# Second part of x fetched in float32 by SyncE and cast by GpSimd, in a convolution and two-layer kernel

## The chip, the cores and the metric

The kernel runs on one core of one Trainium2 chip. The metric is the device time of one execution in microseconds (us), median of several runs; lower is better. The core's engines are TensorE (PE in the profile; PEld is its weight load), VectorE (DVE), ScalarE (ACT), GpSimd (POOL) and SyncE (SP). Transfers between device memory and on-chip memory run on 16 DMA engines. Requests that GpSimd issues appear on queue q0, those of SyncE on queue q1. PSUM is the memory into which TensorE writes.

## The reference, cut to what matters

Each of 8 sequences of 4096 rows of 192 numbers is convolved causally with 7 taps, one set of taps for each of 8 groups of 24 columns; the taps are a softmax. Then each of the 32768 rows goes through a product with w_in (192 by 2048), a leaky ReLU and a product with w_out (2048 by 192).

```python
w = np.exp(weight - max); w = w / (sum(w) + 1e-09)          # 8 heads x 7 taps
x_pad = zeros of 6 rows ahead of x                          # causal
out = np.einsum('hk,bskhg->bshg', w, x_unf)                 # the convolution
h = x @ w_in                                                # (32768, 2048)
g = np.maximum(0.01 * h, h)
return (g @ w_out).astype(np.float32)
```

Everything that a matrix product reads is bfloat16 on the chip; x and the weights arrive as float32.

## The kernel before

Sequences are taken in pairs: the two of a pair (called e = 0 and 1) share the 128 partitions, 64 columns of each in one chunk, with 3 chunks for the 192 columns. A block is 512 rows of a pair; there are 32 blocks. The first two blocks are split into halves of 256 rows, so the work is a list of 34 groups (line 72), the first four of them halves. For each group the kernel needs x transposed (columns on partitions, the tile xt), convolves it into yt, multiplies with w_in into PSUM (mm1, line 488; tile ph), applies the leaky ReLU on ScalarE into g (line 515), and multiplies with w_out (lines 525 and 588). The main loop (line 670) issues mm1 of group i beside the second product of group i-1 and the convolution of group i+1. One mm1 step is called u below; a half block has 8 of them.

The schedule is manual (line 67): every engine carries out its instructions in the order in which the code issues them, and waits come from data dependencies. One engine's instructions stay in that order, so an instruction that waits holds up all behind it on the same engine.

The start is special, since nothing is there to overlap with:

- Rows 0 to 255 of the first pair (part q = 0) are fetched by SyncE in float32 into x_nat (line 142, two requests), cast by ScalarE and VectorE (line 155) and transposed by TensorE (line 181).
- Part q = 1 (rows 256 to 511) is fetched by GpSimd with a cast on the way, into x_rows[1] (line 145, two requests, one for each e); part q = 2 likewise. TensorE transposes them against the identity (line 167). The twelve transposes of part 1 stand inside the very first mm1 step, between its second and third chunk (lines 501 and 502), and VectorE copies their result to xt (line 195).
- Part q = 3 is fetched by GpSimd in six requests (line 149) and transposed by DMA requests of SyncE (line 199).
- w_in comes in five requests of GpSimd (line 316): rows 0 to 127 of the first 1024 columns; then rows 128 to 191 of their nearer and their farther half; then the same two row ranges of the last 1024 columns. VectorE and ScalarE copy parts of it between the two halves of the partitions (spread_up and spread_down, lines 326 and 322), because mm1 needs them there. w_out comes in two requests (line 350).

GpSimd's order at the start is: a mask called sel, w_in rows 0 to 127, the identity (two instructions), w_in nearer half, the two requests of x part 1, three requests of w_in, two of x part 2, two of w_out, two small operations that make the tap weights wk (lines 445 and 446), the six requests of x part 3, and then x for the later blocks (line 96). VectorE uses wk first in the convolution of group 1 (line 222). SyncE's order is: two requests for x part 0, then the DMA transposes of part 3.

The pool stage_pool, from which x_nat comes, has two buffers; before the change one of them is used.

Of the kernel before, what the change touches and what calls it, by code (L numbers as in the profile page):

```python
# [10 lines left out]
FP32 = mybir.dt.float32  # L11
BF16 = mybir.dt.bfloat16
# [3 lines left out]
def kernel(  # L16
# [8 lines left out]
    nc = tc.nc  # L25

    B, S, D = x.shape
# [13 lines left out]
    HS = SUB // 2  # L41
    NFC = F // 128
# [3 lines left out]
    RUN = 4  # L46
# [10 lines left out]
    const_pool = ctx.enter_context(tc.tile_pool(name="const", bufs=1))  # L57
    stage_pool = ctx.enter_context(tc.tile_pool(name="stage", bufs=2))
# [17 lines left out]
    x_nat, x_bf, xt = {}, {}, {}  # L76

    def sync(after, first, why):
        tc.add_manual_dep(
            after.ins, first.ins.name,  # L80
            mybir.DependencyInfo(
                mybir.DependencyClass.Sync, mybir.DependencyReason.DATA
            ),
            reason=why,
        )
# [36 lines left out]
    def new_xt(rp):  # L122
# [10 lines left out]
    x_rows = {  # L133
        q: const_pool.tile([128, 2, HS, D], BF16, name=f"x_rows{q}") for q in (1, 2)
    }

    def load_first(q):
        rows = x[0:2, q * HT : (q + 1) * HT, :].rearrange("e (s p) d -> p e s d", s=HS)
        if q == 0:
            x_nat[q] = stage_pool.tile([128, 2, HS, D], FP32, name="x_nat")  # L140
            for s in range(HS):
                nc.sync.dma_start(out=x_nat[q][:, :, s], in_=rows[:, :, s])
        elif q in x_rows:
            for e in range(2):
                nc.gpsimd.dma_start(out=x_rows[q][:, e], in_=rows[:, e])  # L145
        else:
            for c in range(NCH):
                for e in range(2):
                    nc.gpsimd.dma_start(  # L149
                        out=x_half[q][:, c, :, e, :],  # L150
                        in_=rows[:, e, :, c * CH : (c + 1) * CH],
                    )

    def cast_first(q, s, copy, e=slice(0, 2)):
        copy(  # L155
            out=x_half[q][:, :, s, e, :],
            in_=x_nat[q][:, e, s, :].rearrange("p e (c k) -> p c e k", c=NCH),
        )
# [76 lines left out]
    def y_of(grp, c):  # L235
        blk, t0, T = grp
        if blk not in yt:
            yt[blk] = yt_pool.tile([128, NCH, ST], BF16, name="yt")
        return yt[blk][:, c, t0 : t0 + T]
# [47 lines left out]
    w9 = const_pool.tile([H, K + 1], FP32, name="w9")  # L287
    nc.scalar.dma_start(out=w9[:, 0:K], in_=weight)  # L288
    load_first(0)

    ones = nc.const_aps.tensor(1.0, [128, ST], BF16)
# [7 lines left out]
    for sign, off in ((1, 0), (-1, GRP - 1)):  # L299
        nc.gpsimd.affine_select(  # L300
            out=sel[:, :, 0, :], in_=sel[:, :, 0, :], compare_op=mybir.AluOpType.is_ge,
            fill=0.0, base=off, channel_multiplier=-sign * GRP,
            pattern=[[sign * CH, NCH], [sign, CH]],
# [10 lines left out]
    def load_w_in(n, rows, cols=slice(0, WF)):  # L314
        ps, slot = ((0, 128), 0) if rows == 0 else ((0, CH), 2)
        nc.gpsimd.dma_start(  # L316
            out=w_in[n][ps[0] : ps[1], slot, cols],
            in_=moe_w_in[rows : rows + ps[1], n * WF + cols.start : n * WF + cols.stop],
        )
# [15 lines left out]

    load_w_in(0, 0)
    ident = const_pool.tile([128, 128], BF16)
    make_identity(nc, ident)
    load_w_in(0, 128, near)
    load_first(1)  # L340
    load_w_in(0, 128, far)
    for rows in (0, 128):
        load_w_in(1, rows)
    load_first(2)


    w_out = const_pool.tile([128, NFC, D], BF16)
    for h in range(2):
        cs = slice(h * NFC // (2 * RUN), (h + 1) * NFC // (2 * RUN))
        nc.gpsimd.dma_start(  # L350
            out=w_out.rearrange("p (c i) d -> p c i d", i=RUN)[:, cs],
            in_=moe_w_out.rearrange("(c p i) d -> p c i d", p=128, i=RUN)[:, cs],
        )


    wa = psum_h.tile([128, 2, ST], FP32, name="warm", tag="ph")
# [1 line left out]
    def warm(n, cols=HT, to=wa[:, 0]):  # L358
# [10 lines left out]
        out=nmax, in_=w9[:, 0:K], axis=mybir.AxisListType.X,  # L369
# [3 lines left out]
        out=w9[:, 0:K], in_=w9[:, 0:K], func=mybir.ActivationFunctionType.Exp,  # L373
# [18 lines left out]
    def select(out, parts):  # L392
# [10 lines left out]
    wps_hm = wps_hm[:, :, 0]  # L403
    new_xt(0)
    cast_first(0, 0, nc.scalar.copy)
    cast_first(0, 1, nc.scalar.copy, slice(0, 1))
    cast_first(0, 1, nc.vector.tensor_copy, slice(1, 2))
    taps = const_pool.tile([128, NCH, 2, K + 1, 2], BF16, name="taps")
    nc.vector.tensor_copy(
        out=taps, in_=wps_hm[..., None].to_broadcast([128, NCH, 2, K + 1, 2])  # L410
# [5 lines left out]
    def diag_wide(c, p):  # L416
# [22 lines left out]
        out=rsum, in0=wml[:, :, K:], scalar=1e-9, in1=taps[:, :, 0, K:, 0],  # L439
# [14 lines left out]
    def act_scale(out, in_, scale):  # L454
# [11 lines left out]
        out=y_of(groups[0], 0), in0=hi[:, :HT], scalar=rsum[:, 0, :], in1=low,  # L466
# [301 lines left out]
```

## Time and the profile before

| What | Value |
|---|---|
| Runs of the kernel before | 681.44, 681.47 and 680.72 us, median 681.44 |
| Span of the profiled execution, first to last instruction | 679.2 us |
| Busy in that span: PE, ACT, DVE, POOL | 674.9, 517.6, 481.2, 147.4 us |
| Granted TensorE clock | 1.00 over the span |
| GpSimd's requests for x part 1, issued | from 3.62 us, 1.44 us for the two |
| The same, issue to landing | 3.9 and 3.7 us |
| SyncE's requests for x part 0, issue to landing | 2.6 us each |
| w_out, issue to landing | 7.7 us and 8.8 us |

The profiled execution's own time is its span and what lies around it; against the median of the runs, the part outside the span is 2.2 us. Times in the profile count from the first instruction. Of an instruction, the row of the timeline gives start, duration, engine, line, operation, the tile written and read, the number of instructions merged into the row and, in brackets, the idle time of the engine before it with what ended it.

### The profile page before, as it was taken

Reading aid. Unit: us, or ns where it says so; the run is one execution under the profiler, and the core shown is the slowest. Engines: PE = TensorE matmul, PEld = TensorE weight load, DVE = VectorE, ACT = ScalarE, POOL = GpSimd, SP = SyncE. Lnnn points to the kernel's source line nnn. Section 1 sums busy time; section 2 is a strip of 40 time slices with the busy share of each in tenths; the row PEclk is TensorE's granted clock in tenths of the full one; section 3 lists DMA queues with packets and bytes.
Section 4 is the critical chain, followed back from the end, with each engine's and each line's share of the span. In section 5 each row is a group of like instructions: output and inputs, shape, how many; then the busy total and the mean of one; then the engine's idle time right before and its main releaser. Section 6 shows DMA issues by size and latency. Waiting matters only on the chain.

```text
span 679.2 us, 27092 instructions
## 1 busy us (share of the span) xinstructions
PE 674.9 (99%) x12442; PEld 446.3 (66%) x12442; DVE 481.2 (71%) x816; ACT 517.6 (76%) x601; POOL 147.4 (22%) x208
## 2 busy tenths in 40 slices
PE   9999999999999999999999999999999999999998
PEld 6997666666666666666666666666666666666667
DVE  7989477866768766778667687667786676876612
ACT  7899877777787777777777777778777777777781
POOL 8455221122211222211222112222022220000000
PEclk9999999999999999999999999999999999999999
DMA  9999755655737656556556566567365573321123
GB/s 149 99 119 104 52 85 83 84 64 67 96 74 93 76 54 86 84 85 86 66 63 92 80 92 78 56 83 94 73 87 69 60 96 71 72 56 33 34 49 94
DMA packets 213970, 53.27 MB, mean 78 GB/s; under 512 B 209312, under 2 KB 213536, under 8 KB 213856
## 3 DMA queue, kind: packets, MB, share of 16 engines
q0 software_dynamic: 98832, 13.97, 30.3%
q1 hardware_dynamic: 115008, 37.57, 28.0%
q8 instruction: 97, 1.59, 0.9%
q14 instruction: 17, 0.14, 0.1%
q10 hardware_dynamic: 16, 0.00, 0.0%
HBM read 28.31 MB, written 25.17 MB: 79 GB/s over the span
## 4 chain that ended last, share of the span: by engine, by line
PE 98%; DVE 1%; ACT 0%; issue 0%; ACTq 0%
PE ph L507 49%; PE acc L588 44%; PE po L525 5%; PE acc L259 0%; DVE diag L420 0%; PE ptr L167 0%; ACT L366 0%; ACTq L288 0%; DVE w_in L322 0%; DVE yt L465 0%; DVE o_sb L638 0%; DVE x_half L155 0%; ACT w L372 0%; DVE w_in L326 0%; ACT junk L366 0%
## 5 line engine op out<-in xcount | busy, mean ns | idle before, releaser
L515 ACT ACTIVATE g<-ph 128x1024 bf16<-128x1024 f32 x512 | 496.6, 1021 | 139.8 <-PE ph L507 139.6
L228 DVE SCALAR_TENSOR_TENSOR yt<-xt,wk,yt 128x512 bf16<-128x512 bf16 (+1 forms) x582 | 380.1, 715 | 0.2
L507 PE MATMUL ph<-yt,w_in 64*64 64x512 bf16 (+2 forms) x6048 | 377.5, 369 | 0.3 <-DVE yt L465 0.3
L588 PE MATMUL acc<-g,w_out 64*64 64x512 bf16 x5568 | 339.9, 376 | 0.0
L507 PEld LDWEIGHTS <-w_in 64*64 64x64 bf16 (+1 forms) x6048 | 229.7, 131 | 103.4 <-issue 1.1
L588 PEld LDWEIGHTS <-w_out 64*64 64x64 bf16 x5568 | 178.2, 118 | 118.8
L96 POOL DMA_DIRECT2D x_bf<-in_x_dram x180 | 133.9, 774 | 407.6 <-DMA xt<-x_bf 405.6
L610 DVE STREAM_TRANSPOSE o_t<-acc 128x512 f32<-128x512 f32 x87 | 72.9, 875 | 182.2 <-PE acc L588 182.2
L525 PE MATMUL po<-w_out,g 64*128 64x192 bf16 (+1 forms) x640 | 36.8, 243 | 0.0
L525 PEld LDWEIGHTS <-g 64*128 64x128 bf16 (+1 forms) x640 | 32.6, 95 | 3.2 <-issue 0.4
L222 DVE TENSOR_SCALAR yt<-xt,wk 128x512 bf16<-128x512 bf16 (+1 forms) x97 | 28.8, 320 | 2.4 <-DMA xt<-x_bf 2.4
L598 ACT COPY junk<-junk 128x1 f32<-128x1 f32 x58 | 11.1, 191 | 4.1
L638 DVE COPY o_sb<-po 128x192 f32<-128x192 f32 x8 | 2.8, 356 | 6.8 <-PE po L525 3.9
L638 ACT COPY o_sb<-po 128x192 f32<-128x192 f32 x16 | 5.1, 323 | 0.3
L259 PE MATMUL acc<-xt,diag 64*64 64x256 bf16 x126 | 4.7, 272 | 0.1
L149 POOL DMA_DIRECT2D x_half<-in_x_dram x6 | 4.3, 732 | 0.9 <-DMA w_in<-in_moe_w_in_dram 0.9
L259 PEld LDWEIGHTS <-diag 64*64 64x64 bf16 x140 | 3.7, 106 | 1.0 <-issue 0.4
L360 PE MATMUL warm<-const-bfloat16-1.0 128*128 128x512 bf16 (+2 forms) x8 | 3.3, 577 | 0.8 <-PEq L752 0.8
L145 POOL DMA_DIRECT2D x_rows<-in_x_dram x4 | 2.9, 746 | 0.0
L316 POOL DMA_DIRECT2D w_in<-in_moe_w_in_dram x5 | 2.9, 593 | 0.0
L360 PEld LDWEIGHTS <-const-bfloat16-1.0 128*128 128x128 bf16 x10 | 1.2, 128 | 2.2 <-issue 2.2
L326 DVE COPY w_in<-w_in 64x512 bf16<-64x512 bf16 (+1 forms) x7 | 2.3, 337 | 0.2
(52 smaller groups left out, 25.9 us busy)
## 6 DMA issues: line engine op xcount, KB each, us to landing
out_dram<-o_t SPq DMA_DIRECT2D x112, 192.0 KB, 4.7
x_bf<-in_x_dram POOLq DMA_DIRECT2D x180, 64.0 KB, 3.1
out_dram<-o_sb SPq DMA_DIRECT2D x8, 192.0 KB, 2.8
xt<-x_bf SPq DMA_TRANSPOSE x90, 3.2
w_out<-in_moe_w_out_dram POOLq DMA_DIRECT2D x2, 384.0 KB, 8.3
out_dram<-o_t SPq DMA_DIRECT2D x8, 96.0 KB, 2.4
out_dram<-o_sb SPq DMA_DIRECT2D x8, 96.0 KB, 1.7
w_in<-in_moe_w_in_dram POOLq DMA_DIRECT2D x2, 256.0 KB, 5.5
```

Of the source, the lines that this page charges most:

```text
L96: ins = nc.gpsimd.dma_start(out=t[:, c, :, e, :], in_=src[2 * rp + e, :, :, c * CH : (c + 1) * CH],)
L222: lambda s=src, d=dst, c=c: nc.vector.tensor_scalar_mul(d, s, wk[:, c, 0:1])
L228: lambda s=src, d=dst, c=c, k=k: nc.vector.scalar_tensor_tensor(out=d, in0=s, scalar=wk[:, c, k : k + 1], in1=d, op0=mybir.AluOpType.mult, ...
L259: lambda k=k, p=p, a=a, ps=ps, to=to, acc=accs[e]: nc.tensor.matmul(out=acc[to, :T], lhsT=diag[c][ps, p, k, :], rhs=xt[0][ps, c, a : a + T ...
L360: nc.tensor.matmul(out=to[:, 0:cols], lhsT=ones[:, 0:128], rhs=ones[:, 0:cols], start=True, stop=True,)
L507: nc.tensor.matmul(out=ph[m : m + M, e, i * T : (i + 1) * T], lhsT=w_in_of(f, e, c, m, m + M), rhs=y[ps, c, t0 : t0 + T], start=(c == chun ...
L515: act = nc.scalar.activation(out=g[blk][:, nf * u : nf * (u + 1), :, t0 : t0 + T], in_=ph.rearrange("p e (i t) -> p i e t", i=nf), func=my ...
L525: return nc.tensor.matmul(out=po[m], lhsT=g[b][ps, fc, e, s * 128 : (s + 1) * 128], rhs=w_out[ps, fc, :], start=start, stop=stop,)
L588: ins = nc.tensor.matmul(out=acc2[gi, r][e * CH : (e + 1) * CH, 0:T], lhsT=w_out_of(ps, fc, r), rhs=g[b][ps, fc, e, t0 : t0 + T], start=fi ...
L598: seal = nc.scalar.copy(out=junk, in_=junk)
L610: nc.vector.transpose(out=osb[gi, 0][:, 0 : T // GB, :, r], in_=acc2.pop((gi, r))[:, 0:T].rearrange("p (j k) -> p j k", k=GB),)
L638: ins = copy(out=o_sb[:, n % 2, :], in_=po.pop(n))
```

## The change

Part 1 of x is no longer fetched by GpSimd with a cast. SyncE fetches it in float32 into a second x_nat buffer, in two requests, one for each e; the first of them waits until GpSimd has finished the identity. GpSimd then casts it into x_rows[1] in two instructions of 128 partitions by 384 elements. In GpSimd's order these casts stand behind its requests for w_in and for x part 2, and ahead of its two requests for w_out, which follow them as before. The requests for w_in and x part 2 thus move up by the two requests that are gone. The identity is made by the same two instructions as before, written out, so that their handle can be waited for.

```diff
-    def load_first(q):
+    def load_first(q, after=None):
...
+        elif q in (1,):
+            x_nat[q] = stage_pool.tile([128, 2, HS, D], FP32, name="x_nat")
+            for e in range(2):
+                ins = nc.sync.dma_start(out=x_nat[q][:, e], in_=rows[:, e])
+                if e == 0:
+                    sync(ins, after, "behind a nearer part")
         elif q in x_rows:
             for e in range(2):
                 nc.gpsimd.dma_start(out=x_rows[q][:, e], in_=rows[:, e])
...
     load_w_in(0, 0)
     ident = const_pool.tile([128, 128], BF16)
-    make_identity(nc, ident)
+    after = nc.gpsimd.memset(ident, 0.0)
+    after = nc.gpsimd.affine_select(
+        out=ident, in_=ident, compare_op=mybir.AluOpType.not_equal, fill=1.0,
+        base=0, pattern=[[-1, 128]], channel_multiplier=1,
+    )
+    load_first(1, after)
     load_w_in(0, 128, near)
-    load_first(1)
     load_w_in(0, 128, far)
     for rows in (0, 128):
         load_w_in(1, rows)
     load_first(2)
...
     cast_first(0, 1, nc.vector.tensor_copy, slice(1, 2))
+    for e in range(2):
+        nc.gpsimd.tensor_copy(out=x_rows[1][:, e], in_=x_nat[1][:, e])
+    w_out = const_pool.tile([128, NFC, D], BF16)
+    for h in range(2):
...
+        nc.gpsimd.dma_start(
+            out=w_out.rearrange("p (c i) d -> p c i d", i=RUN)[:, cs],
+            in_=moe_w_out.rearrange("(c p i) d -> p c i d", p=128, i=RUN)[:, cs],
+        )
     taps = const_pool.tile([128, NCH, 2, K + 1, 2], BF16, name="taps")
```

The lines that make w_out are the ones that stood before behind load_first(2). On TensorE, VectorE and ScalarE neither the instructions nor their order change.

More of the change, by code (lines that the diff above doesn't have):

```diff
@@ L154, in cast_first @@
     def cast_first(q, s, copy, e=slice(0, 2)):
-        copy(
+        return copy(
             out=x_half[q][:, :, s, e, :],
@@ L344 @@
     load_first(2)
[L347 to L353, printed above, removed]
     wa = psum_h.tile([128, 2, ST], FP32, name="warm", tag="ph")
@@ L407 @@
     cast_first(0, 1, nc.vector.tensor_copy, slice(1, 2))
+    for e in range(2):
+        nc.gpsimd.tensor_copy(out=x_rows[1][:, e], in_=x_nat[1][:, e])
+    w_out = const_pool.tile([128, NFC, D], BF16)
+    for h in range(2):
+        cs = slice(h * NFC // (2 * RUN), (h + 1) * NFC // (2 * RUN))
+        nc.gpsimd.dma_start(
+            out=w_out.rearrange("p (c i) d -> p c i d", i=RUN)[:, cs],
+            in_=moe_w_out.rearrange("(c p i) d -> p c i d", p=128, i=RUN)[:, cs],
+        )
     taps = const_pool.tile([128, NCH, 2, K + 1, 2], BF16, name="taps")
```

## The prediction

> **What bounds the kernel now.** I read the chain of waits first, since it tells which engine's work sets the end. TensorE has 98% of it; from its first product with w_in at 8.09 us on, the chain never leaves TensorE. So a change at the start counts only as far as it moves that beginning, or opens a hole in TensorE's work behind it. This is the chain at that place (start, duration, what):
>
> ```profile
> 7.56 0.49 DVE yt L465
> 8.05 0.04 issue
> 8.09 0.63 PE ph L507 x8
> 8.72 0.46 PE ptr L167 x12
> 9.18 1.00 PE ph L507 x16
> ```
>
> The twelve transposes of x part 1 (ptr, L167) stand in the middle of the first step and start at 8.72. TensorE works in order, so if part 1 comes late, all behind it moves by the same amount. Before the change its second request landed at 4.35 + 3.7 = 8.05 us, 0.67 us ahead of need.
>
> Next the timeline of GpSimd, whose queue the change rearranges:
>
> ```profile
> 2.85 0.29 POOL masks.py:199 TENSOR_SCALAR_AFFINE_SELECT ident<-ident 128x128 bf16<-128x128 bf16 x1
> 3.10 0.54 POOL L316 DMA_DIRECT2D w_in<-in_moe_w_in_dram  x1
> 3.62 1.44 POOL L145 DMA_DIRECT2D x_rows<-in_x_dram  x2
> 5.03 1.67 POOL L316 DMA_DIRECT2D w_in<-in_moe_w_in_dram  x3
> 6.64 1.48 POOL L145 DMA_DIRECT2D x_rows<-in_x_dram  x2
> 8.05 1.48 POOL L350 DMA_DIRECT2D w_out<-in_moe_w_out_dram  x2
> 9.46 0.32 POOL L445 TENSOR_TENSOR wk<-taps,wml 128x21 f32<-128x21 bf16 x1
> ```
>
> The reader sees a queue without a gap. The identity ends at 3.14, so SyncE's requests can start at about 3.2.
>
> Third, the DMA view of two stretches, 2.0 to 3.8 us (x part 0 by SyncE) and 4.4 to 6.4 us (queue, packets, MB, share of 16 engines):
>
> ```profile
> q1 hardware_dynamic: 532, 0.38, 73.4%
> ...
> q0 software_dynamic: 394, 0.27, 104.5%
> ```
>
> In the second stretch GpSimd's queue alone fills the 16 engines. The new requests bring 0.39 MB into exactly this time. Last, the waits of 8 to 18 us show what could be gained:
>
> ```profile
> DVE w_in L322 <- DMA w_in<-in_moe_w_in_dram: 0.6, 1, 0.6
> PEld L507 <- DVE w_in L326: 0.2, 1, 0.2
> ```
>
> VectorE waits 0.6 us for the late columns of w_in, TensorE 0.2 us for VectorE's copies.
>
> **The change part by part.** *Removed:* two issues on GpSimd, 1.44 us. The three w_in requests start at 3.64 in place of 5.03, those for x part 2 at 5.3 in place of 6.64, and all ends at about 6.7. None of the work before 8.09 gains: there VectorE is busy from 6.67 back to back and has its w_in at 1.87 + 4.5 = 6.4. The gain lies in the two waits above: 0 at least, if something else holds the place; 0.8 at most. I take 0.3, nearer to TensorE's own wait.
>
> *Added on SyncE:* a wait until 3.14 and two issues of 0.45 us each (the row of part 0 has 0.96 us for two). Behind them on SyncE stand only the transposes of part 3, which start at 18.12. This costs nothing; it would if the wait lasted 14 us.
>
> *Added transfer:* when does part 1 land? Lower end: 2.6 us from issue, as part 0 took on idle engines; issued at 3.65, the second request lands at 6.3. Upper end: the new queue takes turns, one piece for one piece, with a full q0. A place where both queues work with small pieces is 64.2 to 64.6 us (q1 stores 768-byte pieces, q0 loads):
>
> ```profile
> q1 hardware_dynamic: 101, 0.07, 74.6%
> q0 software_dynamic: 138, 0.02, 66.2%
> ```
>
> That is 0.73 pieces of q1 for one of q0, whatever their size: q1 is not served first. Part 1 has 512 pieces (part 0's count above, without the few small completion packets), starting at about 4.5: part 0 was issued at 0.81 and its pieces flow from 2.1. By then q0 has moved 0.04 MB (the first stretch) and 0.7 us at 149 GB/s (0.67 MB from 3.6 to 8.1), 0.14 MB together. w_in has 448 rows, one piece each, 71 of them gone; 377 are left with 0.64 MB, and 135 pieces of x part 2 make the 512: 0.05 MB. So 0.69 MB at 149 GB/s is 4.6 us, and part 1's own 0.39 MB takes 1.0 us at its best slices' 390 GB/s, 1.7 us at the stretch's mean of 236. The landing is 4.5 + 4.6 + 1.0 to 1.7 = 10.1 to 10.8. At 0.73 to one, 190 more small pieces go ahead, 0.07 MB or 0.5 us: 11.3. The nearest row is the one with both queues at work, so I take 10.3; the ends are 6.3 and 11.3.
>
> [...]
>
> *Added on GpSimd:* two casts of 128x384 elements. There is no such row. Two affine selects give a slope: 355 ns for 192 elements (mean of L300), 287 ns for 128, so 1.06 ns an element and 0.56 us for 384. Lower end by memset, 258 and 228 ns for the same sizes: 0.35 us. Upper end 1.0 us, if the 0.32 us of the tiny L445 is mostly fixed cost and comes on top. I take 0.56, nearest in kind. The first cast (e = 0) lies in the shadow of the second request; the second one is on the path.
>
> A copy of w_in by VectorE took 0.36 us at 9.88, beside GpSimd's arithmetic, and 0.29 us elsewhere: 0.07 us is the lower price of the two engines meeting; 0.56, one whole cast, the upper. With a late landing VectorE is idle then or reads PSUM; I take 0. [...]
>
> *Sum:* landing 10.3, cast 0.56, signals 0.05: part 1 is ready at 10.9 in place of needed at 8.72, so 2.2 us of hole, less 0.3 us of gain: +1.9 us. On the profiled execution that makes a span of 681.1; with 2.2 us around it 683.3 us, against the median of 681.44.
>
> *What moves behind the casts on GpSimd.* w_out is issued at 10.9 in place of 8.05, 2.8 us later. Its halves landed at 8.05 + 7.7 = 15.8 and 8.8 + 8.8 = 17.6; even with the full delay they land at 18.6 and 20.4, while TensorE, itself 1.9 us later, reads them from 17.29 + 1.9 = 19.2 and 19.26 + 1.9 = 21.2. That cover is 0.6 us; if it were gone, its excess would be added one for one. wk comes at about 12.9 in place of 10.1, where VectorE needs it at 10.26 + 1.9 = 12.2: 0.7 us, which the 0.6 us wait for w_in at 12.21 nearly takes up. Part 3's requests run 2.7 us later; its transposes then end near 26 rather than 23.3, and VectorE uses it from 25.65 + 1.9 = 27.5.
>
> **The rivals.** Changes below 0.2%, 1.36 us, are about what measurement can't tell from none.
>
> *Part 1 comes in time.* If q1 gets several pieces for each of q0, it lands before about 8 us, the casts end by 8.6, and only the 0.3 us gain is left: 681.1 us, not slower. For it: part 0's slices reached 390 GB/s, and a 2 KB piece of w_in is far longer than a 768-byte one, so a fair share by time would help. Against it: the counts at 64 us.
>
> *w_in pays in its place.* If q1 is served first, the first w_in request, 4.5 us to landing, gets 1.0 to 1.7 us later: 7.4 to 8.1. VectorE's copy, due at 6.67, then waits 0.7 to 1.4 us and the first product with it, less 0.3: 681.8 to 682.5. It decides as soon as w_in lands behind 6.67. For it: the bytes must go somewhere in a full stretch. Against it: nothing here shows q1 served first.
>
> *Relief.* If every wait of the first group behind 8.09 went (0.6 and 0.2, and 1.2 us in which ScalarE waits for TensorE, partly the same time), with part 1 in time, up to 1.4 us: 680.0. Against it: those steps are paced by ScalarE's 1 us an activation, which stay.
>
> **How the numbers follow.** The late landing has 0.60; five sixths of it lie above 1.36 us. In time 0.27, w_in pays 0.09, relief 0.04. Slower is 0.50 from the first and 0.04 from the others (w_in's upper end, meeting engines); the same 0.10 + 0.26 + 0.06 = 0.42; faster 0.04, relief alone. The time is 683.3. The range: downward to 681.1, the case in time; upward 684.6, a landing at 11.3 with a cast of 0.85, 12.2 against 8.72, less 0.3. The late case's own range is 682.2 to 684.6.
>
> **What would show it.** Transposes of L167 that start near 10.9 behind an idle TensorE ended by a GpSimd cast, whose own wait was ended by x_nat's transfer; a landing of x_nat's second request more than 5.5 us from its issue; wk and w_out later by 2 to 3 us. I am wrong if the casts run at 6.7 to 8 us without a wait, or if TensorE's first product with w_in itself starts later than 8.2.

## The result, and the profile after

The changed kernel takes 685.69 us (median of 5 runs, 685.47 to 686.81) against 681.13 us for the kernel before (680.67 to 681.47): 1.0071 times as long, 95% interval 1.0059 to 1.0083, or 4.6 us more. The forecast was 683.3 with 681.1 to 684.6: the right direction, and too little. The profiled execution has a span of 684.3 us, 5.1 more than before.

The chain of waits of the changed kernel at the start (start, duration, what) now leads through part 1 of x:

```profile
3.16 0.37 SPq L146
3.53 0.04 issue
3.57 7.90 DMA x_nat<-in_x_dram
11.47 0.05 issue
11.52 0.52 POOL x_rows L410
12.04 0.04 issue
12.08 0.85 PE ptr L173 x10
12.93 1.83 PE ph L517 x16
14.76 1.05 PE acc L265 x23
15.81 1.43 PE ph L517 x24
```

SyncE asks for the second half of part 1 (e = 1) at 3.57 us and gets it 7.9 us later. The cast takes 0.5 us, and eleven of the twelve transposes begin at 12.08 in place of 8.72 (one, which needs the first half alone, ran at 9.91). The reader should also compare the durations behind them with the chain of before: 0.46 us for the transposes and 1.00 for the sixteen products then, 0.85 and 1.83 now. The same instructions take nearly twice as long. The table by stretches of the changed kernel shows why (stretch, its length, busy time and instructions of each engine, granted TensorE clock, DMA share, GB/s):

```profile
8.80:12.00 3.20, 0.26 (x2) 0.11 (x1) 1.14 (x3) 0.66 (x2) 0.98 (x3) 0.98 1.00 160
12.20:15.20 3.00, 3.00 (x39) 1.99 (x43) 2.02 (x6) 1.43 (x2) 2.91 (x6) 0.50 0.66 95
15.40:17.00 1.60, 1.60 (x40) 1.37 (x32) 1.55 (x4) 0.80 (x2) 1.60 (x3) 1.00 1.14 195
```

TensorE was busy for 0.26 of 3.20 us, and then worked from 12.2 to 15.2 at half the clock. GpSimd's timeline in the changed kernel shows the two waits in front of the casts, and all that is queued behind them:

```profile
3.09 2.14 POOL L322 DMA_DIRECT2D w_in<-in_moe_w_in_dram  x4
5.19 1.47 POOL L151 DMA_DIRECT2D x_rows<-in_x_dram  x2
9.36 0.50 POOL L410 CAST x_rows<-x_nat 128x384 bf16<-128x384 f32 x1 [2.69 <-DMA x_nat<-in_x_dram]
11.52 0.51 POOL L410 CAST x_rows<-x_nat 128x384 bf16<-128x384 f32 x1 [1.66 <-DMA x_nat<-in_x_dram]
11.97 1.41 POOL L414 DMA_DIRECT2D w_out<-in_moe_w_out_dram  x2
13.38 0.25 POOL L455 TENSOR_TENSOR wk<-taps,wml 128x21 f32<-128x21 bf16 x1
```

In the profiled executions the account is this. The transposes start 12.08 - 8.72 = 3.36 us later. From there to the mm1 steps that start at 19.92 before and at 24.56 after, it took 24.56 - 12.08 = 12.48 us against 11.20: 1.28 us more, while the clock was halved. Together 4.64 us. The other half microsecond of the 5.1 lies behind that point (659.7 against 659.3 us). In two executions with the same work behind the start, c_before and c_after below, that remainder was 659.4 and 659.6; I take it for scatter.

### The profile page after: what moved, and what is told of

It is laid out like the page before. It is cut to its first block, busy times and chain, and to the rows that moved or that the text cites. A ratio compares the mean times of both kernels' runs of the same rounds, so it can differ in the third digit from the quotient of the medians.

```text
span 684.3 us, 27094 instructions
## 1 busy us (share of the span) xinstructions
PE 676.9 (99%) x12442; PEld 448.6 (66%) x12442; DVE 482.3 (70%) x816; ACT 517.8 (76%) x601; POOL 146.9 (21%) x208
## 4 chain that ended last, share of the span: by engine, by line
PE 98%; DMA 1%; POOL 0%; issue 0%; SPq 0%; DVE 0%; POOLq 0%
PE ph L517 49%; PE acc L598 44%; PE po L535 5%; DMA x_nat<-in_x_dram 1%; PE acc L265 0%; PE ptr L173 0%; POOL sel L306 0%; POOL w_in L322 0%; POOL x_rows L410 0%; SPq L146 0%; DVE o_sb L648 0%; POOL ident L345 0%; POOL sel L304 0%; POOL ident L344 0%; POOLq L345 0%
## 5 line engine op out<-in xcount | busy, mean ns | idle before, releaser
L228 DVE TENSOR_SCALAR yt<-xt,wk 128x512 bf16<-128x512 bf16 (+1 forms) x97 | 30.4, 341 | 3.1 <-ACT g L525 2.8
L608 ACT COPY junk<-junk 128x1 f32<-128x1 f32 x58 | 11.1, 192 | 4.1
L173 PE MATMUL ptr<-ident,x_rows 128*64 128x128 bf16 x24 | 1.6, 265 | 3.0 <-POOL x_rows L410 3.0
```

The costliest lines, as they stand in the source:

```text
L228: lambda s=src, d=dst, c=c: nc.vector.tensor_scalar_mul(d, s, wk[:, c, 0:1])
L608: seal = nc.scalar.copy(out=junk, in_=junk)
```

## The experiments

All kernels below have every DMA transpose (x part 3 and the later blocks) replaced by a plain copy of the same bytes on the same queue; x is not transposed there, so that part of the result isn't computed. The first of them starts at 18 us or later, behind the place in question.

```diff
-            ins = nc.sync.dma_start_transpose(
+            ins = nc.sync.dma_start(
```

The times, against the kernel before as it stands, in the same chip session:

| Run | Median us (range) | Ratio, 95% interval | Part 1, second request: issue to landing |
|---|---|---|---|
| c_before | 681.23 (680.66 to 681.60) | 1.0000, 0.999 to 1.001 | by GpSimd |
| c_after | 686.49 (684.04 to 687.62) | 1.0075, 1.0053 to 1.0097 | 7.5 us |
| e1b_no_wait | 681.88 (680.90 to 682.18) | 1.0009, 1.0000 to 1.0019 | 6.0 us |
| e2b_keep_busy | 684.97 (684.55 to 685.23) | 1.0057, 1.0042 to 1.0072 | 7.8 us |
| e3b_casts_first | 684.51 (683.95 to 685.23) | 1.0045, 1.0029 to 1.0062 | 4.8 us |
| e4b_long_pieces | 684.77 (683.11 to 685.89) | 1.0050, 1.0033 to 1.0067 | 6.2 us |
| e5b_all_partitions | 683.46 (682.88 to 686.95) | 1.0039, 1.0025 to 1.0052 | 5.9 us |
| e6_both | 682.18 (681.60 to 682.48) | 1.0015, 1.0005 to 1.0024 | 5.6 us |
| e7_far_upper | 681.18 (680.87 to 681.61) | 1.0004, 0.9995 to 1.0012 | by GpSimd |

**The two bases.**

> The kernel before with every DMA transpose (x part 3 and all later blocks) replaced by a plain copy of the same bytes on the same queue, so that x is convolved there without having been transposed: the common base of the experiments. The first such transpose starts at 18.1 us and TensorE sets the pace throughout, so all theories expect the time of the kernel before, 681.1 plus or minus 0.7, with the first product with w_in near 8.1 us and the transposes of part 1 near 8.7 us.

> The changed kernel in the same plain-copy form. All theories: the start is as in the changed kernel (second request of part 1 lands near 11.4 us, transposes of part 1 near 12.1, half clock for 3.4 us), and the time is 4 to 5 us above the plain-copy form of the kernel before.

The time of c_before is as expected, though in its profile the first product with w_in starts at 8.59 us and the transposes at 9.50, later than expected (the last section has the reason). c_after was expected 4 to 5 us above c_before and is 5.3 above; its second request landed at 11.07 us and not near 11.4, and the half clock is missing from its profile. The late landing is there, so the plain copies leave the cause in place. And c_after brought something the changed kernel had not shown: its four executions lie 3.6 us apart, and they order themselves by the mean granted clock: 684.04 us at 1.000, 685.75 at 0.997, 687.23 and 687.62 at 0.995. The profile is of the first of these. The chain of waits of c_after:

```profile
3.57 7.51 DMA x_nat<-in_x_dram
11.07 0.05 issue
11.13 0.52 POOL x_rows L406
11.64 0.04 issue
11.69 0.52 PE ptr L171 x11
12.21 1.00 PE ph L513 x16
13.21 0.78 PE acc L261 x24
```

Nearly the same landing, a shorter hole (TensorE waited 1.9 us for the second cast here; in the changed kernel 1.1 and 1.9 us for the two), and behind it the durations of the kernel before: 1.00 and 0.78 us. So the late landing and the clock are two separate losses.

What went with the second one can be read from the clock record that each trace holds. In all eleven traces every stretch of that record but the last, which the end cuts off, is a whole multiple of 3.41 us (in the changed kernel two of them at full clock from 5.05 us on, then one at half clock), and it begins at another moment in each execution, from 4.08 to 6.73 us. Cut into windows of that length, the starts of the changed kernel, of c_after and of e3b_casts_first below look like this (columns as in the table by stretches):

```profile
8.46:11.87 3.41, 0.60 (x5) 0.20 (x4) 1.39 (x3) 1.00 (x2) 0.85 (x2) 1.00 1.01 164
11.87:15.28 3.41, 3.20 (x39) 2.19 (x43) 2.10 (x6) 1.50 (x2) 3.32 (x7) 0.50 0.68 97
```

```profile
6.73:10.14 3.41, 2.87 (x73) 2.10 (x65) 2.01 (x6) 2.45 (x5) 0.50 (x1) 1.00 0.91 170
10.14:13.55 3.41, 1.86 (x43) 1.58 (x47) 0.91 (x3) 1.00 (x3) 2.34 (x5) 1.00 0.72 87
```

```profile
13.28:16.69 3.41, 1.69 (x37) 1.12 (x27) 3.09 (x8) 1.13 (x2) 3.41 (x6) 1.00 1.15 164
16.69:20.10 3.41, 3.41 (x39) 1.78 (x37) 2.99 (x7) 2.10 (x3) 1.74 (x3) 0.50 1.43 156
```

The windows in which TensorE was busy for 0.60 and 1.69 of 3.41 us were followed by half clock. In the eleven traces every full window with 1.69 us or less was, and none with 1.86 us or more. In c_after the border at 10.14 cut the hole in two, and 1.86 us of work were left in the window behind it. I read from this that it depends on where the windows lie against the hole whether the loss comes; that differs from execution to execution, as the clocks of c_after do (0.995 to 1.000).

**Fill the hole with work.** In front of the twelve transposes of part 1, inside transpose_first:

```diff
+            for n in range(84 if q == 1 else 0):
+                nc.tensor.transpose(
+                    out=t[n % 2 * CH : (n % 2 + 1) * CH, 0, 0, :],
+                    in_=ident[:, 0:CH], identity=ident,
+                )
```

> The changed kernel (plain-copy form) with 84 transposes of the identity, 38 ns each, put ahead of the transposes of part 1, so that TensorE works through most of the hole (3.2 us); their result is overwritten. Theory (the granted clock halves at 12.1 us because TensorE had been idle, and costs half of 3.2 us): clock 1.00 throughout, the steps behind the hole take 2.3 us again and not 3.7, time 1.6 us (1.3 to 1.9) below the changed kernel in plain-copy form. Rival (the steps behind the hole are slow because GpSimd and VectorE are late): the time stays.

The timeline of TensorE in this run:

```profile
8.85 2.54 PE L170 MATMUL ptr<-ident 128*64 128x128 bf16 x84
11.22 0.22 PE L176 MATMUL ptr<-ident,x_rows 128*64 128x128 bf16 x1
12.01 0.52 PE L176 MATMUL ptr<-ident,x_rows 128*64 128x128 bf16 x11 [0.57 <-POOL x_rows L411]
12.46 0.85 PE L518 MATMUL ph<-yt,w_in 64*128 64x256 bf16 x12
13.76 0.41 PE L518 MATMUL ph<-yt,w_in 64*128 64x256 bf16 x4 [0.44 <-issue]
```

The part lands as late as ever (transposes at 12.01), but the transposes take 0.52 us and not 0.85, and the mean clock is 0.999 to 1.000 in all four executions. Of the nine executions in which part 1 came as late and nothing filled the hole (five of the changed kernel, four of c_after), eight show 0.995 to 0.998. The median falls by 1.5 us, in the range forecast, though the two intervals overlap; the values of the clock, not the medians, carry this verdict. In the window from 8.92 to 12.33 us TensorE carried out transposes alone, 2.84 us of them, and these kept the clock. The gain was not full: TensorE stood another 0.44 us at 13.3, for which the profile names no releaser.

**Take the wait for the identity away.**

```diff
-                if e == 0:
+                if e == 0 and after is not None:
...
-    load_first(1, after)
+    load_first(1)
```

> The changed kernel (plain-copy form) without SyncE's wait for the identity: its two requests for x part 1 go out right behind those of part 0, at about 1.7 and 2.2 us. Theory (part 1 is late because its pieces take turns with w_in's pieces, which flow from 3.6 us): with 1.4 us of head start most of part 1 is through before w_in begins; it lands at 4.5 to 5.5 us, GpSimd casts without a wait at about 6.7 to 7.7, no hole and no half clock; w_in's first request pays up to 1.2 us. Time 0.1 below to 1.3 us above the base. Rival (SyncE's queue is slow beside GpSimd's whenever it starts): landing still behind 8 us, time more than 2 us above the base.

The cost is nearly gone: 681.88 us, no execution below a clock of 0.999. But the landing is not what the theory said. The requests went out at 1.80 and about 2.25 us, and the second landed 6.0 us after issue, near 8.2, not at 4.5 to 5.5. Head start or not, it needed much of the stretch. GpSimd waited 1.14 us for it and cast from 7.80 to 8.8, just in time. What was paid was part 0, with which it shares SyncE's queue: the chain of waits has

```profile
1.29 3.58 DMA x_nat<-in_x_dram
4.87 0.02 issue
4.89 0.35 DVE x_half L159
```

so the second request of part 0 landed at 4.87 where it had landed near 3.9 before. The rival, that the queue is slow at any time, has the landing behind 8 us right, but not the time (0.6 us above the base, not 2), and 6.0 is less than 7.5.

**Take competing requests away.**

```diff
-    for rows in (0, 128):
-        load_w_in(1, rows)
-    load_first(2)
...
     for e in range(2):
         nc.gpsimd.tensor_copy(out=x_rows[1][:, e], in_=x_nat[1][:, e])
+    for rows in (0, 128):
+        load_w_in(1, rows)
+    load_first(2)
```

> The changed kernel (plain-copy form) with the requests for the last 1024 columns of w_in and for x part 2 behind the casts: until part 1 has landed, GpSimd's queue holds only three requests of w_in. Theory (competition with the pieces of GpSimd's queue): the second request of part 1 lands 4 to 5 us from issue in place of 7.5, at 7.5 to 8.6 us; transposes start at 8.2 to 9.3, clock 1.00. What it loses: those columns of w_in are asked for at about 8.5 and land near 13 to 14.5, needed at about 12.5. Time 0.5 to 2.5 us above the base of 681.2. Rival (the transfer is slow by itself or by the moment of its issue): landing still 10.5 or later, and the time is 6 us or more above the base, since more is late.

With the same issue at 3.16 and 3.57 us, the second request now takes 4.8 us. So neither the moment of issue nor the transfer itself makes it late, but what GpSimd's queue carries beside it. The time does not profit: it is 3.3 us above the base, beyond the 2.5 expected. TensorE has a new hole later on:

```profile
15.71 2.10 PE L513 MATMUL ph<-yt,w_in 64*128 64x256 bf16 x23 [1.72 <-DVE w_in L328]
```

Not because the moved columns of w_in land late, as was expected: they landed 3.3 and 3.9 us after their issue, by about 13.3 us, and VectorE copied them at 14.77 without a wait for them. VectorE itself was late. GpSimd now issues six requests, 4 us, between the casts and the tap weights wk, and VectorE waited for wk:

```profile
12.81 0.27 POOL L451 TENSOR_TENSOR wk<-taps,wml 128x21 f32<-128x21 bf16 x1
13.41 0.29 DVE L224 TENSOR_SCALAR yt<-xt,wk 128x256 bf16<-128x256 bf16 x1 [2.56 <-POOL wk L452]
14.77 0.42 DVE L324 COPY w_in<-w_in 64x1024 bf16<-64x1024 bf16 x1
```

This hole lost clock too: two of the four executions had 0.997 and 0.998 where 1.00 was expected, and the profile, of one of these, shows the half clock from 16.69 us.

**Fewer pieces.**

```diff
+            runs = x[0:2, q * HT : (q + 1) * HT, :].rearrange("e (p s) d -> p e s d", s=HS)
...
-                ins = nc.sync.dma_start(out=x_nat[q][:, e], in_=rows[:, e])
+                ins = nc.sync.dma_start(out=x_nat[q][:, e], in_=runs[:, e])
```

> The changed kernel (plain-copy form) with part 1 fetched in 256 pieces of 1536 bytes in place of 512 of 768 (two neighbouring rows to a partition), so its 512 rows stand in another order. Same bytes, half the pieces. Theory (turns are piece for piece): it needs half as many turns; the second request lands 4.5 to 6 us from issue, at 8 to 9.6; time 1 to 3 us above the base. Rival (shares by bytes, or the total work of the slowest engine decides): landing 7.1 to 7.9 us from issue as before, time 3 to 6 us above the base.

7.5 us became 6.2, a little above the range of the theory and outside that of the rival. The hole shrank to 1.1 us of waiting in the profiled execution, the one at a clock of 1.000, which took 683.11 us. The other three still lost clock (0.997 and 0.998; their holes aren't on record), so the median stands at 684.77, 3.5 us above the base: more than the theory had, and in the rival's range. Only 3 entries of part 1 are left behind 9.0 us here.

**Even load.** In load_w_in, for rows 128 to 191:

```diff
+    for n in range(NPW):
+        nc.vector.memset(w_in[n][0:CH, 2, :], 0.0)
...
+        if rows:
+            rows, ps = 0, (0, 128)
+            cols = slice(cols.start, (cols.start + cols.stop) // 2)
```

> The changed kernel (plain-copy form) with the three requests for rows 128 to 191 of w_in, which fill 64 partitions, replaced by requests of the same bytes that fill 128 partitions with half as many columns (the first rows of w_in, so those parts of the product are not computed), and two small memsets on VectorE. Theory (a transfer into 64 partitions keeps only half of the 16 DMA engines, and part 1 waits in turn on those): with the load spread evenly the second request of part 1 lands 5.5 to 6.5 us from issue, near 9.5; time 1 to 3.5 us above the base. Rival (all 16 engines share every transfer, so the spread makes no difference): 7.1 to 7.9 us from issue as before, time 3 to 6 us above the base.

5.9 us, in the range of the theory. But the edit changes two things: with half the columns each piece of these requests is half as long, and there are twice as many (256 in place of 128 for the first two). Even load or shorter pieces beside part 1: this run can't tell which. The DMA view of the stretch from 9.0 to 11.5 us tells how the delay had looked. First c_after, in which part 1 landed at 11.07, then e5b_all_partitions, in which it landed at 9.52 (queue, pieces, MB, share of 16 engines):

```profile
q0 software_dynamic: 581, 0.41, 108.0%
q1 hardware_dynamic: 47, 0.03, 5.1%
```

```profile
q0 software_dynamic: 698, 0.38, 113.5%
...
q1 hardware_dynamic: 2, 0.00, 0.2%
```

In c_after nine tenths of part 1 are through at 9.0 us, and the landing waits two more microseconds for the last 47 entries. With the edit there is no such tail. Seven of eight executions kept a clock of 1.000. That a request into 64 partitions loads only some of the DMA engines, and that the tail sits on these, was my assumption; no run shows it, since the profile doesn't number the engines.

**Both together.**

> Both edits together in the changed kernel (plain-copy form): part 1 in 256 pieces of 1536 bytes, and the 64-partition requests of w_in spread over 128 partitions with half the columns; rows of part 1 stand in another order, and rows 128 to 191 of w_in are not the ones multiplied. Theory (few turns on an evenly loaded set of engines): alone the edits took 1.3 and 1.6 us off the landing of 7.5 us; together the second request lands 4.2 to 5.2 us from issue, near 8.2, the casts end near 8.8, a hole of 0.3 us at most, clock 1.00 in all executions; time 0 to 0.8 us above the base. Rival (both edits remove the same delay): landing 5.7 to 6.2 us from issue, time 1.7 to 2.5 us above the base.

The second request took 5.6 us, between the two expectations and nearer to the rival's; so the two edits mostly remove the same delay, the tail: no entry of part 1 is left behind 9.0 us. The hole was down to 0.4 us:

```profile
9.12 0.24 PE L172 MATMUL ptr<-ident,x_rows 128*64 128x128 bf16 x1
9.76 0.52 PE L172 MATMUL ptr<-ident,x_rows 128*64 128x128 bf16 x11 [0.40 <-POOL x_rows L412]
```

All ten executions kept the clock (0.999 or 1.000), and the time is 1.3 us above that session's median of the kernel before (680.86).

**Even load in the kernel before**, as a version that might beat both. That the edit evens the load of the DMA engines was again an assumption, which no run shows. With it the farther half of rows 128 to 191 of w_in goes into partitions 64 to 127 and is copied down in place of up; the product is the same:

```diff
+        up = CH if rows and n == 0 and cols == far else 0
...
-            out=w_in[n][ps[0] : ps[1], slot, cols],
+            out=w_in[n][up + ps[0] : up + ps[1], slot, cols],
...
-                    spread_up(0, slice(2, 3), far)
+                    nc.vector.tensor_copy(
+                        out=w_in[0][0:CH, 2, far], in_=w_in[0][CH:128, 2, far]
+                    )
```

> [...] Theory (uneven load delays what TensorE waits for): w_in's last columns land up to 1 us earlier, VectorE's wait of 0.6 us goes, time 0.1 to 0.5 us below the base. Rival (at the start of the kernel before, ScalarE and TensorE set the pace whatever VectorE waits for): within 0.2 us of the base.

681.18 us against 680.86, no gain, though VectorE's wait of 0.6 us is gone from the profile (c_before, whose start was late, does not show it either); the rival holds, 0.1 us beyond its range. No version that I ran is faster than the kernel before.

## Why the prediction was wrong, point by point

*Which row sets the end:* right. The transposes inside the first mm1 step moved, and all behind them moved with them; the first product with w_in itself did not start later (7.91 us). The chain does leave TensorE at the start now, for part 1's transfer.

*The landing of part 1:* the step that failed first. I took 10.3 us and gave 11.3 as the upper end; it was 11.4 (11.07 in c_after). That the number is so near is partly luck, since the working behind it was wrong. It let 512 pieces of q0 go ahead in turns, at least one for each piece of part 1, 0.69 MB. The changed kernel's DMA view from 5.0 to 9.0 us shows two pieces of q1 for one of q0, and bytes nearer to equal than pieces:

```profile
q0 software_dynamic: 242, 0.27, 54.0%
q1 hardware_dynamic: 494, 0.36, 36.9%
```

So nine tenths of part 1 were through at 9.0 us, sooner than the sum would have it, although its pieces flowed only from 5.1 us and not from 4.5. What the sum had nothing for is the end: it divided bytes by a rate of all 16 DMA engines together, as if they finished together; but the last tenth took two microseconds more, with its last entry at 11.1 us and the landing at 11.47. That this comes of what GpSimd's queue carries beside it is shown by e3b_casts_first (4.8 us from issue, against 7.5 in c_after). What makes the tail is open: it goes with half as many pieces in part 1 (e4b_long_pieces, 1.3 us less), and with w_in spread and its pieces halved (e5b_all_partitions, 1.6 us less), and the two do not add up in e6_both. A slip stands in the text of the prediction besides: the row at 64 us, which it calls the nearest, gives 11.3 by its own working and not the 10.3 taken.

The hole that came of it was 3.36 us in place of 2.2 between the profiles of the two kernels. Between c_before and c_after it was 11.69 - 9.50 = 2.19, since TensorE was late at the start in both of these.

*The cast:* 0.50 and 0.51 us against the estimate of 0.56. Right. The 0 for VectorE and GpSimd meeting, and its upper end of a whole cast, were estimates of mine, not shown before the change. In the changed kernel VectorE's copy of w_in beside the first cast, from 9.39 us, took 0.61 us, and the one before it, at 8.55, took 0.29; TensorE was waiting for part 1 then.

*The clock:* the second step that failed, a term left at nothing. I had read a granted clock of 1.00 throughout and treated it as fixed. In the profiled execution the half clock cost 1.28 us, and it is what put the time out of the range: c_after's one execution without it took 684.04 us, inside 681.1 to 684.6, and those at 0.995 took 3.2 to 3.6 us more. A window of 3.41 us at half clock takes 0.0025 off the mean clock of such a run (half of 3.41 in 684 us), so 0.997 and 0.998 are one such window and 0.995 is two. In the changed kernel the half clock lasted from 11.87 to 15.28 us, one window of 3.41 us behind the one with the hole; where the hole was filled, in e2b_keep_busy, the mean clock stayed at 0.999 to 1.000. A shorter wait went with half clock too: 1.72 us in e3b_casts_first, with TensorE busy in half of the window (1.69 of 3.41 us).

*The gain of 0.3 us from earlier w_in requests:* not there. From the first transposes to the same later step, e1b_no_wait, where nothing was late, took 20.75 - 9.65 = 11.10 us, c_before 20.49 - 9.50 = 10.99 and the kernel before 11.20. VectorE's 0.6 us wait for w_in is in the last of these alone, so without it 0.1 to 0.2 us is won at most, and the time of e7_far_upper, where it is gone too, shows no gain. In the changed kernel VectorE even had a new wait of 0.7 us for the nearer half of w_in.

*Covers behind the casts:* they held. w_out was issued at 11.97, later than the 10.9 of the prediction, yet landed 4.5 to 6.1 us from issue, while the DMA engines were busy for only half of the time (49% from 11.5 to 13 us); TensorE read it from 21.93 without a wait. For wk VectorE waited 0.4 us in c_after, and TensorE did not notice.

*The rivals:* part 1 in time did not happen in the changed kernel; e1b_no_wait is close to it and came out at 1.0009 times, not below. w_in paying in its place did not happen either: the first request kept 4.4 us, and only the nearer half came late, unseen behind the hole. What paid in e1b_no_wait was part 0, which I had not thought of.

The sum with measured terms: 3.36 of hole, 1.28 of clock, no gain: 4.64 against the 1.9 predicted and the 4.6 measured. The terms are read from two single profiles, whose starts scatter by 0.8 us, so the close agreement with the medians is partly luck.

## What to carry to other kernels

Here the other queue took 1.44 us of issue off GpSimd, but the second request of part 1 then took 7.9 us to land in place of 3.7, beside a queue that in the kernel before filled the 16 engines alone (104.5% from 4.4 to 6.4 us). In such a stretch ask when the last piece comes, not when the bytes would be through. When the late tile stops TensorE for microseconds, price the clock as well as the wait: in c_after the executions that lost clock took 1.7 to 3.6 us more than the one that did not. Before moving a request for the sake of a wait, check that the wait was on the path; here the waits that the change could remove were worth 0.2 us at most. And see what stands behind the moved request in the same engine's order: in e3b_casts_first the tap weights did, and TensorE waited for them in the end.

## What the runs showed of the hardware that was not expected

The start itself scatters by most of a microsecond, and the kernel isn't the cause. In 4.5 to 6.8 us TensorE has the same program in both of these executions, the kernel before and c_before, with the columns as in the table by stretches above:

```profile
4.50:6.80 2.30, 2.25 (x63) 1.90 (x67) 2.25 (x10) 1.40 (x5) 2.30 (x5) 1.00 1.13 140
```

```profile
4.50:6.80 2.30, 2.30 (x37) 1.56 (x38) 2.24 (x10) 0.98 (x3) 2.30 (x5) 1.00 1.04 129
```

63 products in one and 37 in the other; the first product with w_in came at 8.09 and at 8.59 us, the transposes of part 1 at 8.72 and at 9.50. The clock column says 1.00 for both. But the clock record in the trace begins at 4.08 us in the first and only at 6.61 in the second, and there the pace of c_before changes:

```profile
4.50:6.61 2.11, 2.11 (x33) 1.38 (x34) 2.08 (x9) 0.98 (x3) 2.11 (x4) 1.00 1.03 127
6.61:8.50 1.89, 1.89 (x68) 1.69 (x61) 1.32 (x4) 0.94 (x2) 1.89 (x4) 1.00 0.99 122
```

That is 64 ns a product ahead of the record and 28 ns behind its beginning. So the column's 1.00 ahead of the record isn't to be trusted: the pace there is about that of half the clock. Why the record begins where it does is not shown. A difference of half a microsecond between single profiles of such a kernel says nothing; the steps behind the start, and medians of many executions, do.
